# Reordering the front of an attention–MLP kernel around one table load, and finishing the first tiles of each pass in token halves

## The chip, the cores and the metric

The kernel runs on one core of one Trainium2 chip. The metric is the device time of one launch in microseconds (us). Before the change it is 222.36 us, the median of three runs (221.37 to 223.29). The profiled execution of the same kernel spans 220.5 us from its first to its last instruction. All moments below, such as "at 21.91", are us from the start of that span.

A core has five engines that run side by side, each through its own list of instructions in order: TensorE (PE in the profile, and PEld for its weight loads), VectorE (DVE), ScalarE (ACT), GpSimd (POOL) and SyncE (SP, which only issues transfers here). They wait for one another through semaphores.

## What is computed

Two layers follow one another: a chunked attention over four batches of eight heads, and an MLP with a "snake" activation.

```python
# attention: S = 768 tokens in 24 chunks of 32; each chunk sees 16 tokens to its left,
# 8 to its right, and 8 memory rows
scores = (q_c @ k_full.T) / sqrt(64)
out_c  = softmax(scores) @ v_full                 # q, k, v: (4, 8, 768, 64)
x      = out.transpose(0, 2, 1, 3).reshape(3072, 512)

# MLP: d_model 512, d_ff 2048
h = x @ w_in                                      # (3072, 2048)
s = sin(alpha * h)
g = h + s * s / (alpha + 1e-9)
y = g @ w_out                                     # (3072, 512)
```

One batch of 768 tokens is one *pass* of the MLP's first layer, so there are four passes. The 2048 columns of h are cut into 16 *tiles* of 128 (numbered 0 to 15, `ft` in the code). A tile of a pass is 128 partitions by 768 tokens, held as two halves of 384 tokens, each half in a PSUM bank of its own.

## The kernel before

First the work on one tile: eight matmuls into PSUM (four for each token half), the sine on ScalarE, the square on the engine that a letter of a string names (V for VectorE, P for GpSimd, A for ScalarE), and a last step on VectorE that makes g. This last step is called the *snake step* below. It reads the PSUM tile for the last time, so it is also what makes the two banks free for a later tile.

```python
def half_first(hT, ft, hf, xT):                 # 4 matmuls: one token half of one tile
    for kt in range(KT):                        # KT = 4
        nc.tensor.matmul(hT[:, hf, 0:HALF], w_in_sb[:, kt, P * ft:P * ft + P],
                         xT[:, kt, HALF * hf:HALF * hf + HALF], ...)

def ahead(ft, hf, xT):                          # first half of tiles 0 to 2, before the pass
    if ft < 3:
        begun[ft] = two("big")
        half_first(begun[ft], ft, hf, xT)

def first(ft, xT, gT, square, hT=None):
    if hT is None:
        hT = two("h")
        half_first(hT, ft, 0, xT)
    half_first(hT, ft, 1, xT)
    u = mlp.tile([P, 2, HALF], F32, name="u", bufs=4)
    nc.scalar.activation(u[:], hT[:, :, 0:HALF], ACTF.Sin, scale=alpha_sb[:, ft:ft + 1])
    def squared():
        if square == "A":
            nc.scalar.activation(u[:], u[:], ACTF.Square)
        else: ...                               # u * u on VectorE (V) or GpSimd (P)
    def finish():                               # the snake step
        nc.vector.scalar_tensor_tensor(out=gT[:, ft, :]..., in0=u[:],
            scalar=inv_alpha[:, ft:ft + 1], in1=hT[:, :, 0:HALF], op0=ALU.mult, op1=ALU.add)
    return squared, finish
```

The loop of a pass. A snake step is put one tile later in VectorE's list than its tile (two later if GpSimd squares):

```python
for ft in range(FT):
    begin(ft)
    square = squares[ft % len(squares)]
    squared, fin = first(ft, xT, gT, square, begun.pop(ft, None))
    feed.take(...)                              # matmuls of an earlier pass's second layer
    for due, f in [p for p in pend if p[0] <= ft]: f()
    pend = [p for p in pend if p[0] > ft]
    squared()
    pend.append((ft + (2 if square == "P" else 1), fin))
...
layer(0, xT, "VPPAPAVPAVPPAAAA", begin_0, 0)    # pass 0; no second-layer work beside it
layer(i, xT, "VAVAVAVAAVAAVAVA", begin, 0)      # pass 1; none beside it either
layer(i, xT, "AAAV", begin, feed.left() - ...)  # passes 2 and 3, with second-layer matmuls
```

A pass has four pairs of PSUM banks in turn, so tile 4 takes the pair of tile 0, tile 5 that of tile 1, and so on.

The front is the attention of batch 0, worked by pairs of heads and halves of tokens. `sc_half` makes scores and the exponential, `pv` multiplies by v and normalises on VectorE, `x` transposes the result on TensorE and copies it from PSUM to `xT` on ScalarE. `warm(n)` puts n matmuls on zeros into TensorE's list[...]; they write the bank that the next `x` will use. The sine's table has to be loaded on ScalarE between the last exponential and the first sine. The end of the front:

```python
pv(1, 0); sc_half(3, 0); pv(1, 1); sc_half(3, 1)
units = [(hp, half) for hp in range(1, HP - 1) for half in range(2)]
x(1, 0)
nc.scalar.preload_act_table(ACTF.Sin)           # ahead of five more copies on ScalarE
for n in range(2, len(units)):
    pv(*units[n])
    if n == 2:
        warm(2)
    x(*units[n - 1])
warm(1)
pv(3, 0)
x(2, 1)
pv(3, 1)
x(3, 0)
ahead(0, 0, xT)
ahead(1, 0, xT)
x(3, 1)
ahead(2, 0, xT)
```

In the later attentions the table load stands after the last exponential, and `ahead` for tiles 0, 1 and 2 stands among the last transposes.

Of the kernel before, what the change touches and what calls it, by code (L numbers as in the profile page):

```python
# [9 lines left out]
P = 128  # L10
# [4 lines left out]
F32 = mybir.dt.float32  # L15
ACTF = mybir.ActivationFunctionType
ALU = mybir.AluOpType
# [25 lines left out]
def kernel(  # L43
# [12 lines left out]
    nc = tc.nc  # L56
# [5 lines left out]
    HP = H // 2  # L62
# [3 lines left out]
    HALF = S // 2  # L66
# [6 lines left out]
    mlp = ctx.enter_context(tc.tile_pool(name="mlp", bufs=3))  # L73
# [13 lines left out]
    def take_bank(kind):  # L87
        ring = rings[kind]
        bank = next(n for n in ring if n not in kept)
        ring.remove(bank)  # L90
        ring.append(bank)
        return bank

    def two(kind="big"):
        bank = take_bank(kind)
        return ps[:, bank:bank + 2, :]

    def single(kind="one"):
# [27 lines left out]
    alpha_sb = consts.tile([P, FT], F32, name="alpha_sb")  # L126
    inv_alpha = consts.tile([P, FT], F32, name="inv_alpha")
# [132 lines left out]
    def put_k(b, hp, t):  # L260
        kT = kTs[b % 2]
        nc.scalar.copy(  # L262
            kT[:, hp, 72:72 + 7 * 104].rearrange("p (s c) -> p s c", c=104)[:, :, 0:96]
            .rearrange("p s (a r) -> p s a r", r=6),
            t[:, :, 8:120].rearrange("p r (s a) -> p s a r", a=16),
        )
# [66 lines left out]
    def warm(n):  # L333
        z = ps[:, rings["one"][0], :]
        for _ in range(n):
            nc.tensor.matmul(z, idle[:, 0:P], idle[:])  # L336
# [42 lines left out]
        )  # L379
        return x_blk  # L380

    def unit_turn(xT, hp, half, x_blk):
        xtp = packed(single(), 4, QW)
        for jj in range(4):
            nc.tensor.transpose(
                xtp[:, jj, :], x_blk[:, jj].rearrange("p e d -> p (e d)"), ident[0:QW, 0:QW]
            )
        nc.scalar.copy(
            xT[:, hp, HALF * half:HALF * half + HALF].rearrange("p (j c) -> p j c", j=4), xtp
        )  # L390

    def attention_first(kq, alphas, ahead):
        xT = xp.tile([P, KT, S], BF, name="xT")
        pt, xb = {}, {}

        def turn_k(hp):
            t = turn(kq[0], hp, None)
            put_k(0, hp, t)
            put_k_edges(0, hp, t)

        def turn_q(hp):
            put_q(0, hp, turn(kq[1], hp, None))

        def sc_half(hp, half):
            pt[hp, half] = unit_scores(hp, half)

        def sc(hp):
            for half in range(2):
                sc_half(hp, half)

        def pv(*u):
            xb[u] = unit_values(*u, pt[u])

        def x(*u):
            unit_turn(xT, *u, xb.pop(u))

        turn_k(0)
        warm(2)
        turn_q(0)
        mt = packed(single(), HP, 32)  # L420
        for g in range(HP):
            nc.tensor.transpose(mt[:, g, :], memk_bf[0:32, 2 * g:2 * g + 2, :].rearrange("p e d -> p (e d)"), ident[0:32, 0:32])
        nc.vector.tensor_copy(memkT[:], mt)
        put_memk(0)
        warm(3)
        turn_k(1)
        put_memv(0, nc.vector, 0, H)
# [12 lines left out]
        pv(0, 1)  # L440
        t3 = turn(kq[0], 3, None)
        put_k(0, 3, t3)
        warm(1)
        x(0, 0)
        sc_half(2, 0)
        put_k_edges(0, 3, t3)
        turn_q(3)
        sc_half(2, 1)
        x(0, 1)
        warm(1)  # L450
        plan(big=(4, 0, 2))
        pv(1, 0)
        sc_half(3, 0)
        pv(1, 1)
        sc_half(3, 1)
        units = [(hp, half) for hp in range(1, HP - 1) for half in range(2)]
        x(1, 0)
        nc.scalar.preload_act_table(ACTF.Sin)
        for n in range(2, len(units)):
            pv(*units[n])  # L460
            if n == 2:
                warm(2)
            x(*units[n - 1])
        warm(1)
        pv(3, 0)
        x(2, 1)
        pv(3, 1)
        x(3, 0)
        ahead(0, 0, xT)
        ahead(1, 0, xT)  # L470
        x(3, 1)
        ahead(2, 0, xT)
        return xT

    def attention(b, stream, shares, lag, crossed, beside=iter(()), beside_from=0):
# [32 lines left out]
    def half_first(hT, ft, hf, xT):  # L508
        for kt in range(KT):
            nc.tensor.matmul(  # L510
                hT[:, hf, 0:HALF],
                w_in_sb[:, kt, P * ft:P * ft + P],
                xT[:, kt, HALF * hf:HALF * hf + HALF],
                start=(kt == 0), stop=(kt == KT - 1),
            )

    begun = {}

    def ahead(ft, hf, xT):
        if ft < 3:  # L520
            begun[ft] = two("big")
            half_first(begun[ft], ft, hf, xT)

    def first(ft, xT, gT, square, hT=None):
        if hT is None:
            hT = two("h")
            half_first(hT, ft, 0, xT)
        half_first(hT, ft, 1, xT)
        u = mlp.tile([P, 2, HALF], F32, name="u", bufs=4)
        nc.scalar.activation(u[:], hT[:, :, 0:HALF], ACTF.Sin, scale=alpha_sb[:, ft:ft + 1])  # L530

        def squared():
            if square == "A":
                nc.scalar.activation(u[:], u[:], ACTF.Square)  # L534
            else:
                eng = nc.vector if square == "V" else nc.gpsimd
                eng.tensor_tensor(out=u[:], in0=u[:], in1=u[:], op=ALU.mult)  # L537

        def finish():
            nc.vector.scalar_tensor_tensor(  # L540
                out=gT[:, ft, :].rearrange("p (e c) -> p e c", e=2),
                in0=u[:], scalar=inv_alpha[:, ft:ft + 1], in1=hT[:, :, 0:HALF],
                op0=ALU.mult, op1=ALU.add,
            )
        return squared, finish

    def second(i, gT, cut=0):

# [118 lines left out]
    xT = attention_first(kq, alphas, ahead)  # L667
# [14 lines left out]
    def layer(i, xT, squares, begin, to_feed):  # L682
        gT = gTs[i % 2]
        pend = []
        fed = 0
        for ft in range(FT):
            begin(ft)
            square = squares[ft % len(squares)]
            squared, fin = first(ft, xT, gT, square, begun.pop(ft, None))
            want = to_feed * (ft + 1) // FT  # L690
            feed.take(want - fed)
            fed = want
            for due, f in [p for p in pend if p[0] <= ft]:
                f()
            pend = [p for p in pend if p[0] > ft]
            squared()
            pend.append((ft + (2 if square == "P" else 1), fin))
        for due, f in pend:
            f()
        feed.add(second(i, gT, 0 if i else 13), NSUB * FT)  # L700

    prs = []

    def begin_0(ft):
        if ft == 3:
            plan(h=[6] + rings["big"])
        if ft == 12:
            load_v(1)
            send_memv(1)
            send_memv(2)  # L710
        if ft == 15:
            prs.extend(pair_up(kq1[n // HP], n % HP) for n in range(4))
# [6 lines left out]
    for pc in range(2 * HP):  # L719
        hp = pc % HP  # L720
# [12 lines left out]
    xT = attention(1, feed, (6, 8, 4, 4, 4, 3, 3, 3, 3, 1, 1), 2, 5)  # L733

    for i in range(1, B):
# [26 lines left out]
        if not last:  # L762
# [3 lines left out]
            xT = attention(i + 1, feed, (4, 8, 4, 4, 3, 3, 3, 3, 4, 4, 4), 2, 5)  # L766
# [33 lines left out]
```

## Time and profile before

| row of the page or of a view | what it tells |
|---|---|
| PE 209.9 us busy (95%), ACT 147.8 (67%), DVE 136.4 (62%), POOL 83.0 (38%) | TensorE has hardly any idle time over the whole span |
| 80 to 90: PE 9.05, DVE 9.58, ACT 9.49 of 10 us | in pass 1 VectorE and ScalarE are as full as TensorE |
| 120 to 200: PE 20.00 of 20 us in each of the four stretches | from pass 2 on TensorE never stops |
| granted clock of TensorE 0.997 | the clock plays no part |

A row of the timeline gives the start, the time that it lasted, the engine, the line of the kernel, the operation, what it writes and reads, how many instructions were merged into the row, and in brackets how long the engine had stood idle just before and what ended that. A row of the groups gives the busy total and the mean of one instruction in ns. The busy share of an engine is an average over stages with different limits, so the stages have to be read one by one.

### The profile page before, as it was taken

The numbers are of one execution on the slowest core, as the hardware profiler recorded it, in microseconds if no ns is written. First come the engines' busy times: TensorE is split into PE (matmuls) and PEld (weight loads), VectorE is DVE, ScalarE is ACT, GpSimd is POOL, SyncE is SP. The second block draws the span as 40 slices with busy tenths as digits, with TensorE's granted clock in tenths as the row PEclk, the third lists the DMA queues.
The fourth block names the chain that finished last, engine by engine and source line by source line (L and its number), as shares of the span: only waits on it lengthen the run. The fifth ranks groups of instructions, "written<-read, shape, count | busy, mean of one in ns | idle before, by whom it ended". The sixth has DMA issues, their size and how long they took to land.

```text
span 220.5 us, 4412 instructions
## 1 busy us (share of the span) xinstructions
PE 209.9 (95%) x1684; PEld 113.8 (52%) x1684; DVE 136.4 (62%) x234; ACT 147.8 (67%) x217; POOL 83.0 (38%) x102
## 2 busy tenths in 40 slices
PE   7999699999999889999999999999999999999994
PEld 3456455555545555554555555544555555544453
DVE  5867458874527769995872865765854863861110
ACT  2458588895778389999846879797919678660010
POOL 7998653598800599400049179300000000000000
PEclk9999999999999999999999999999999999999998
DMA  5999999999999699996339999996530110101212
GB/s 82 163 165 172 207 207 208 200 174 122 92 198 164 80 159 146 152 175 95 75 86 154 122 110 138 180 218 110 137 116 0 48 52 0 48 37 61 95 48 97
DMA packets 98877, 26.96 MB, mean 122 GB/s; under 512 B 86808, under 2 KB 95912, under 8 KB 98856
## 3 DMA queue, kind: packets, MB, share of 16 engines
q0 software_dynamic: 71520, 14.82, 87.8%
q1 hardware_dynamic: 27336, 11.86, 25.6%
q8 instruction: 13, 0.21, 0.4%
q14 instruction: 8, 0.07, 0.1%
HBM read 29.69 MB, written 6.29 MB: 163 GB/s over the span
## 4 chain that ended last, share of the span: by engine, by line
PE 74%; DVE 10%; DMA 5%; ACT 5%; issue 3%; POOL 1%; DVEq 0%; POOLq 0%
PE ps L556 33%; PE ps L510 27%; DVE gT L540 5%; DMA xT<-x_blk 3%; DVE u L537 3%; PE ps L283 3%; DMA q_bf<-in_q_dram 2%; ACT u L530 2%; PE ps L309 2%; PE ps L579 2%; PE ps L336 1%; PE ps L247 1%; PE ps L341 1%; DVE x_blk L375 1%; PE ps L349 1%
## 5 line engine op out<-in xcount | busy, mean ns | idle before, releaser
L556 PE MATMUL ps<-w_out_sb,gT 128*128 128x512 bf16 x368 | 95.5, 380 | 0.2
L510 PE MATMUL ps<-xT,w_in_sb 128*128 128x384 bf16 x512 | 91.5, 326 | 2.7 <-DVE gT L540 1.3
L540 DVE SCALAR_TENSOR_TENSOR gT<-u,inv_alpha,ps 128x768 bf16<-128x768 f32 x64 | 63.4, 1012 | 24.4 <-ACT u L534 20.8
L530 ACT ACTIVATE u<-ps,alpha_sb 128x768 f32<-128x768 f32 x64 | 56.7, 896 | 27.8 <-PE ps L510 27.1
L510 PEld LDWEIGHTS <-w_in_sb 128*128 128x128 bf16 x512 | 49.4, 98 | 40.9 <-issue 5.8
L556 PEld LDWEIGHTS <-gT 128*128 128x128 bf16 x368 | 32.8, 98 | 29.1 <-issue 0.5
L534 ACT ACTIVATE u<-u 128x768 f32<-128x768 f32 x40 | 33.7, 843 | 1.2
L296 ACT ACTIVATE pt<-ps,biasm 128x256 bf16<-128x256 f32 x72 | 28.7, 473 | 4.6 <-PE ps L283 1.8
L569 DVE COPY o_sb<-ps 128x512 f32<-128x512 f32 x17 | 11.7, 689 | 25.3 <-PE ps L556 25.2
L537 DVE TENSOR_TENSOR u<-u 128x768 f32<-128x768 f32 x18 | 17.1, 952 | 6.0 <-ACT u L530 5.9
L183 POOL DMA_DIRECT2D vw<-in_v_dram x15 | 18.1, 1214 | 0.3 <-issue 0.3
L316 DVE TENSOR_TENSOR x_blk<-ps,rinv 96x512 bf16<-96x512 f32 x24 | 16.5, 687 | 0.8
L143 POOL DMA_DIRECT2D kst<-in_k_dram x16 | 11.1, 691 | 5.2 <-DMA vw<-in_v_dram 5.2
L262 ACT COPY kT<-ps 128x672 bf16<-128x672 bf16 x8 | 5.7, 718 | 9.7 <-PE ps L247 7.2
L571 ACT COPY o_sb<-ps 128x512 f32<-128x512 f32 x6 | 3.5, 584 | 12.7 <-PE ps L556 12.7
L537 POOL TENSOR_TENSOR u<-u 128x768 f32<-128x768 f32 x6 | 9.2, 1546 | 6.5 <-ACT u L530 6.5
L148 POOL DMA_DIRECT2D kst<-in_k_dram x16 | 11.6, 726 | 0.1
L336 PE MATMUL ps<-idle 128*128 128x512 bf16 x27 | 9.0, 448 | 2.3 <-DVE vw L618 1.2
L309 PEld LDWEIGHTS <-pt 128*128 128x128 bf16 x192 | 9.0, 98 | 4.2
L153 POOL DMA_DIRECT2D qst<-in_q_dram x12 | 10.7, 896 | 0.7 <-DMA vw<-memv_st 0.7
L283 PEld LDWEIGHTS <-kT 64*128 64x128 bf16 x192 | 4.9, 94 | 10.4 <-issue 9.9
L315 DVE RECIPROCAL rinv<-ps 96x8 f32<-96x8 f32 x24 | 4.8, 202 | 8.2 <-ACT pt L296 5.2
(81 smaller groups left out, 140.0 us busy)
## 6 DMA issues: line engine op xcount, KB each, us to landing
out_dram<-o_sb SPq DMA_DIRECT2D x23, 256.0 KB
w_out_sb<-in_moe_w_out_dram POOLq DMA_DIRECT2D x2, 1024.0 KB, 18.3
w_in_sb<-in_moe_w_in_dram POOLq DMA_DIRECT2D x3, 512.0 KB, 10.7
vw<-in_v_dram POOLq DMA_DIRECT2D x3, 512.0 KB, 9.2
qst<-in_q_dram POOLq DMA_DIRECT2D x12, 128.0 KB, 6.0
vw<-in_v_dram POOLq DMA_DIRECT2D x2, 448.0 KB, 12.3
kst<-in_k_dram POOLq DMA_DIRECT2D x14, 64.0 KB, 5.3
kst<-in_k_dram POOLq DMA_DIRECT2D x14, 56.0 KB, 5.4
```

The source lines that it names most:

```text
L148: nc.gpsimd.dma_start(kst[72:72 + n, j, :].rearrange("p (h d) -> p h d", d=D), k[b, :, QW * j + 48:QW * j + 48 + n, :].rearrange("h p d -> ...
L183: nc.gpsimd.dma_start(vw[p0:p1, c0:c1, 0:D], flat[r0:r0 + QW * (c1 - c0)].rearrange("(n t) d -> t n d", t=QW)[0:p1 - p0],)
L296: nc.scalar.activation(pt[:, 0:H * QW].rearrange("p (g e c) -> p g e c", g=2, e=4)[:, :, :, 32 * m:32 * m + 32], sc[:, :, 0:4 * QW].rearra ...
L309: nc.tensor.matmul(otv[:, e, hp, :], pt[:, QW * i:QW * i + P], vws[b % 2][:, 2 * hp + e, j, 0:D + 1],)
L316: nc.vector.tensor_tensor(out=x_blk[:].rearrange("p g e d -> p e g d"), in0=otv[0:QW, :, :, 0:D], in1=rinv[:].unsqueeze(3).to_broadcast([Q ...
L510: nc.tensor.matmul(hT[:, hf, 0:HALF], w_in_sb[:, kt, P * ft:P * ft + P], xT[:, kt, HALF * hf:HALF * hf + HALF], start=(kt == 0), stop=(kt ...
L530: nc.scalar.activation(u[:], hT[:, :, 0:HALF], ACTF.Sin, scale=alpha_sb[:, ft:ft + 1])
L534: nc.scalar.activation(u[:], u[:], ACTF.Square)
L537: eng.tensor_tensor(out=u[:], in0=u[:], in1=u[:], op=ALU.mult)
L540: nc.vector.scalar_tensor_tensor(out=gT[:, ft, :].rearrange("p (e c) -> p e c", e=2), in0=u[:], scalar=inv_alpha[:, ft:ft + 1], in1=hT[:, ...
L556: nc.tensor.matmul(ps[:, bank, :], gT[:, ft, P * s:P * s + P], w_out_sb[:, ft, :], start=(ft == 0), stop=(ft == FT - 1),)
L569: nc.vector.tensor_copy(o_sb[:], ps[:, bank, :])
```

## The change

It has two parts. The first moves the load of the sine's table behind the copy of `x(3, 0)`, so that the copies of the front no longer stand behind it in ScalarE's list; the transposes, the value products and the zero matmuls are put in another order (six zero matmuls in this stretch in place of three), `x(3, 1)` is copied by VectorE, and only tiles 0 and 1 are begun ahead of pass 0. The second part lets every tile that is begun ahead of a pass go through sine and square for its first token half at once, both on ScalarE, and through the snake step for that half at the start of the pass; the pass then does only the second half of these tiles. It is meant to bring work forward into time when ScalarE and VectorE are idle, and to shorten what lies between the first matmul of a pass and the first bank that comes free.

```diff
 sc_half(3, 1)
-units = [(hp, half) for hp in range(1, HP - 1) for half in range(2)]
 x(1, 0)
-nc.scalar.preload_act_table(ACTF.Sin)
-for n in range(2, len(units)):
-    pv(*units[n])
-    if n == 2:
-        warm(2)
-    x(*units[n - 1])
+pv(2, 0)
 warm(1)
+x(1, 1)
+pv(2, 1)
+warm(2)
+x(2, 0)
 pv(3, 0)
+warm(2)
 x(2, 1)
 pv(3, 1)
+warm(1)
 x(3, 0)
+nc.scalar.preload_act_table(ACTF.Sin)
 ahead(0, 0, xT)
+x(3, 1, nc.vector.tensor_copy)
 ahead(1, 0, xT)
-x(3, 1)
-ahead(2, 0, xT)
...
 def ahead(ft, hf, xT):
     if ft < 3:
-        begun[ft] = two("big")
-        half_first(begun[ft], ft, hf, xT)
+        hT = two("big")
+        half_first(hT, ft, hf, xT)
+        u = mlp.tile([P, 2, HALF], F32, name="u", bufs=4)
+        e = slice(hf, hf + 1)
+        sine(u, hT, ft, e)
+        nc.scalar.activation(u[:, e], u[:, e], ACTF.Square)
+        begun[ft] = (hT, u)
...
 # first(), squared() and the snake step now work on u[:, e] and hT[:, e]:
 # e is the second half alone for a tile that was begun ahead, else both halves
...
 def layer(i, xT, squares, begin, to_feed):
     ...
+    for ft in sorted(begun):
+        snake(gT, ft, *begun[ft], slice(0, 1))
     for ft in range(FT):
...
 def begin_0(ft):
-    if ft == 3:
-        plan(h=[6] + rings["big"])
+    if ft == 2:
+        plan(h=[rings["big"][0], 6] + rings["big"][1:])
```

The later passes keep their three tiles begun ahead, each with its first half finished early.

More of the change, by code (lines that the diff above doesn't have):

```diff
@@ L380, in unit_values, with unit_turn @@
         return x_blk
-    def unit_turn(xT, hp, half, x_blk):
+    def unit_turn(xT, hp, half, x_blk, copy):
         xtp = packed(single(), 4, QW)
@@ L387, in unit_turn @@
             )
-        nc.scalar.copy(
-            xT[:, hp, HALF * half:HALF * half + HALF].rearrange("p (j c) -> p j c", j=4), xtp
-        )
+        copy(xT[:, hp, HALF * half:HALF * half + HALF].rearrange("p (j c) -> p j c", j=4), xtp)
     def attention_first(kq, alphas, ahead):
@@ L412, in pv, with x @@
             xb[u] = unit_values(*u, pt[u])
-        def x(*u):
-            unit_turn(xT, *u, xb.pop(u))
+        def x(hp, half, copy=nc.scalar.copy):
+            unit_turn(xT, hp, half, xb.pop((hp, half)), copy)
         turn_k(0)
@@ L517, with sine, first, snake @@
     begun = {}
+    def sine(u, hT, ft, e):
+        nc.scalar.activation(u[:, e], hT[:, e, 0:HALF], ACTF.Sin, scale=alpha_sb[:, ft:ft + 1])
     def ahead(ft, hf, xT):
         if ft < 3:
-            begun[ft] = two("big")
-            half_first(begun[ft], ft, hf, xT)
-    def first(ft, xT, gT, square, hT=None):
-        if hT is None:
+            hT = two("big")
[5 more added lines that the diff above has]
+            begun[ft] = (hT, u)
+    def first(ft, xT, square, started=None):
+        e = slice(0, 2)
+        if started is not None:
+            hT, u = started
+            e = slice(1, 2)
+        else:
             hT = two("h")
             half_first(hT, ft, 0, xT)
+            u = mlp.tile([P, 2, HALF], F32, name="u", bufs=4)
         half_first(hT, ft, 1, xT)
-        u = mlp.tile([P, 2, HALF], F32, name="u", bufs=4)
-        nc.scalar.activation(u[:], hT[:, :, 0:HALF], ACTF.Sin, scale=alpha_sb[:, ft:ft + 1])
+        sine(u, hT, ft, e)
         def squared():
             if square == "A":
-                nc.scalar.activation(u[:], u[:], ACTF.Square)
+                nc.scalar.activation(u[:, e], u[:, e], ACTF.Square)
             else:
                 eng = nc.vector if square == "V" else nc.gpsimd
[L537 to L545, printed above, removed]
+                eng.tensor_tensor(out=u[:, e], in0=u[:, e], in1=u[:, e], op=ALU.mult)
+        return hT, u, e, squared
+    def snake(gT, ft, hT, u, e):
+        nc.vector.scalar_tensor_tensor(
+            out=gT[:, ft, :].rearrange("p (e c) -> p e c", e=2)[:, e],
+            in0=u[:, e], scalar=inv_alpha[:, ft:ft + 1], in1=hT[:, e, 0:HALF],
+            op0=ALU.mult, op1=ALU.add,
+        )
     def second(i, gT, cut=0):
@@ L688, in layer @@
             square = squares[ft % len(squares)]
-            squared, fin = first(ft, xT, gT, square, begun.pop(ft, None))
+            hT, u, e, squared = first(ft, xT, square, begun.pop(ft, None))
             want = to_feed * (ft + 1) // FT
@@ L693, in layer @@
             for due, f in [p for p in pend if p[0] <= ft]:
-                f()
+                snake(gT, *f)
             pend = [p for p in pend if p[0] > ft]
             squared()
-            pend.append((ft + (2 if square == "P" else 1), fin))
+            pend.append((ft + (2 if square == "P" else 1), (ft, hT, u, e)))
         for due, f in pend:
-            f()
+            snake(gT, *f)
         feed.add(second(i, gT, 0 if i else 13), NSUB * FT)
```

## The prediction, made before the changed kernel was run

> **What bounds the kernel now.** I read the busy shares of the stretches first, to see which engine limits which stage; then the chain of work that ended last, through the front and the first pass; then TensorE's timeline in pass 1; and last the groups, for the price of one instruction of each kind.
>
> ```profile
> 80.00:90.00 10.00, 9.05 (x54) 5.02 (x53) 9.58 (x12) 9.49 (x12) 10.00 (x15) 1.00 2.10 143
> 90.00:100.00 10.00, 9.94 (x64) 5.56 (x64) 9.42 (x11) 9.56 (x13) 0.63 (x2) 1.00 1.53 161
> 120.00:140.00 20.00, 20.00 (x114) 11.01 (x113) 14.18 (x16) 16.64 (x21) 14.05 (x19) 1.00 2.37 129
> ```
>
> The columns are the busy us of PE, PEld, DVE, ACT and POOL. In pass 1 (75 to 101) VectorE and ScalarE are full. From 120 to 200 TensorE alone is full, in each stretch of 20 us, so there time can go only with TensorE's work, and the change takes none away from passes 2 and 3. What it can win lies before 101.
>
> ```profile
> 21.91 1.28 ACT L458
> 23.20 0.49 ACT xT L388
> 23.73 0.38 PE ps L336
> 24.71 0.70 DVE x_blk L375
> 25.46 0.36 PE ps L385 x4
> 25.84 0.49 ACT xT L388
> 26.37 0.97 PE ps L510 x5
> 27.51 1.32 PE ps L510 x8
> 28.85 0.91 ACT u L530
> 29.79 0.97 DVE u L537
> 30.86 1.02 DVE gT L540
> 31.93 5.47 PE ps L510 x32
> ```
>
> This is the chain at the front's end. The load of the sine's table is on it: the copies of x stand behind it, a zero matmul waits 1.11 us for their bank, then value product, normalising and the last copies follow. At 28.85 the first sine starts; sine, square and snake step of tile 0, each on 768 columns, take until 31.87, and tile 4, which needs tile 0's banks, starts at 31.93. TensorE had stood 0.51 us.
>
> ```profile
> 77.34 3.41 PE L510 MATMUL ps<-xT,w_in_sb 128*128 128x384 bf16 x20 [0.22 <-DVE xT L329]
> 81.25 5.67 PE L510 MATMUL ps<-xT,w_in_sb 128*128 128x384 bf16 x32 [0.50 <-DVE gT L540]
> 89.98 7.96 PE L510 MATMUL ps<-xT,w_in_sb 128*128 128x384 bf16 x48 [0.15 <-DVE gT L540]
> ```
>
> In pass 1 TensorE runs from 77.34 to 97.94, 20.60 us for the 116 matmuls left after the three halves ahead. One takes 0.163 us in a stream (24 in 4.07 us at 27.35, of which about 0.33 is the last one's whole length), so 18.9 us of work and 1.7 of waiting for VectorE's snake steps.
>
> ```profile
> L540 DVE SCALAR_TENSOR_TENSOR gT<-u,inv_alpha,ps 128x768 bf16<-128x768 f32 x64 | 63.4, 1012 | 24.4 <-ACT u L534 20.8
> L530 ACT ACTIVATE u<-ps,alpha_sb 128x768 f32<-128x768 f32 x64 | 56.7, 896 | 27.8 <-PE ps L510 27.1
> L534 ACT ACTIVATE u<-u 128x768 f32<-128x768 f32 x40 | 33.7, 843 | 1.2
> L537 DVE TENSOR_TENSOR u<-u 128x768 f32<-128x768 f32 x18 | 17.1, 952 | 6.0 <-ACT u L530 5.9
> ```
>
> These are the prices of a whole tile: snake step 1012 ns, sine 896, square 843 on ScalarE and 952 on VectorE (GpSimd 1546).
>
> [...] The trace has the 1283 (the row at 21.91) [...]: the next copy starts at 23.20, 0.01 us after the load's end. So I count 1.28 us and no more. [...] the trace has 896 and 843. So half a tile costs more than half: [...] 320 ns less, which is 576 ns for a sine and 523 for a square (estimates from 896 and 843). [...] the trace has 952. For 384 I take 400 ns off: 552 for a square, and 612 for a snake step (from 1012). [...] The two halves of a tile lie in two banks, so TensorE may fill one while ScalarE reads the other. No run yet shows this overlap inside one tile.
>
> **The front, step by step.** I lay the new order on the durations above. Up to 21.2 nothing changes. Then, with no table load in the way: copy (1,1) on ScalarE ends at 22.35, where the old trace has 23.7; pv(2,1) and two zero matmuls end at 22.4, as copy (1,0) freed their bank at 21.90; x(2,0) at 22.4, its block being ready at 22.23; pv(3,0) at 22.56; two zero matmuls, then x(2,1) at 23.2; pv(3,1) at 23.4; x(3,0) at 24.05, when its block is normalised. VectorE's normalisations, 0.93 us a pair of instructions, are now the steps that the rest waits for. Copy (3,0) ends at 24.95 instead of 26.32: 1.37 us earlier, the 1.28 of the load and a little. The three extra zero matmuls (0.21 us each) lie in gaps.
>
> Then the load, 24.95 to 26.23, stands before the first sine. Meanwhile TensorE does tile 0's first half (its last matmul waits for copy (3,0), as before), x(3,1), tile 1's first half (to 26.0), the second halves of tiles 0 and 1 (x(3,1) copied by VectorE at 25.86), and tiles 2 and 3 whole, done at 29.9 instead of 31.42.
>
> ScalarE after the load, at about 0.53 us for each half operation in a row: sine and square of tile 0's half, the same for tile 1, then the second-half sines: tile 0's ends near 28.95, tile 1's near 29.5, whole sine 2 at 30.4, sine 3 at 31.3. Square of half 0 on VectorE 0.55, snake half 0.61: banks of tile 0 free at 30.2. Tile 4 starts at about 30.25, where TensorE was ready at 29.9. Against 31.93 that is **1.7 us earlier**. ScalarE itself is only 1.0 us earlier (sine 3 ends 31.3 against 32.35), since it has two squares more (1.05 us) and two sines in halves (2 x 576 - 896 = 256 ns each), but it has 1.8 us of waits for TensorE between 33 and 44 to make that up.
>
> Through the rest of pass 0 the waits stay about the same: in the old trace 96 matmuls took 16.27 us where a stream needs 95 x 0.163 + 0.33 = 15.8. In the new order the bank of tile 2 (whole square on GpSimd, 1.55 us, done near 32.05) costs 0.3 us at tile 6. I put the end of pass 0 **1.5 us earlier**, at 46.6.
>
> **Between the passes.** The attention of batch 1 begins with turned k and q. The transfer of q was issued at 24.63 and took 26.2 us to land, so it lands at 50.8 whatever the engines do; GpSimd first reads it at 52.97. A gain of up to 2.1 us passes; 1.5 does. The load of v lands at about 59.4, and its last part is first read at 64.65. The sum stays 1.5 us.
>
> **Pass 1.** Shown on the old clock. The table is loaded by 73.89 and ScalarE idles until 78.18, so three half sines and squares fit in: tile 0's half is in PSUM at 75.26, tile 2's at 77.11; the six operations end near 78.6. VectorE does the three half snake steps between 77.3 and 79.2, where it had almost nothing. In the pass proper VectorE then has, instead of 16 snake steps and 7 squares (16 x 0.95 + 7 x 0.88 = 21.4 us in its stream), 13 whole and 3 half steps, 5 whole and 2 half squares: 12.4 + 1.7 + 4.4 + 1.0 = 19.5. That is 1.9 less. ScalarE has 13 whole and 3 half sines, 8 whole and 1 half squares from 78.6: about 13 x 0.85 + 3 x 0.53 + 8 x 0.83 + 0.5 = 19.8, ending at 98.4; in the old trace it ends at 99.83. So VectorE stops being the limit, ScalarE becomes it, and TensorE's waits (1.7 us) nearly vanish. The next attention's first exponentials come **1.4 us earlier**, as do the matmuls.
>
> **Passes 2 and 3.** TensorE-bound: nothing won. ScalarE's extra work, three squares and three split sines in each, about 2 us, falls after the exponentials, where it waits 5.0 us for TensorE (117.77 is its first sine). **0 us.**
>
> Sum: 1.5 + 1.4 + 0 = 2.9 us of 222.36, which is **219.4 us**.
>
> **The rivals.** First, ScalarE takes the place of VectorE and of the load: the moved load now stands straight before the first sine, and ScalarE gets about 1.5 us more work in pass 0. For it speaks that ScalarE is busy 20 of 22 us there. Against it speaks the 1.8 us of slack. If it ruled, pass 0 would win 0.7 us and pass 1 perhaps 0.8: 220.9. Second, the time won in pass 0 is given back at a transfer: q of batch 1, or the crossings of k and q for batch 2, which SyncE issues one after another until 102.03. For it speaks that neither moves with ScalarE. Against it, q has 2.1 us to spare, and the crossings are released by x of the pass before, so they shift with it, and the last is used after 109. It would leave about 1.4 of the sum: 221.0. Third, it goes better: the shorter first path takes out all of the 0.45 us of waits in pass 0 and all of 1.7 in pass 1, with the front's whole 1.7: 1.7 + 0.4 + 1.7 = 3.8, 218.6. Beyond 2% (217.9) I'd need a gain after 101, where TensorE is full.
>
> **Range and chances.** The three rivals span 218.6 to 221.0; the three runs of before differ by 1.9 us, so I widen by about 0.6 below and 0.3 above: 218.0 to 221.3. Faster by over 2% needs all that the third rival gives and 0.7 us more: 0.12. Slower by over 2% needs a new wait of 7 us, for which I see no source: 0.03. Within 2%: 0.85.
>
> **What would show it.** Right: the table load near 24.9 with no zero matmul waiting for a copy; tile 4 at 30.0 to 30.5; second-layer matmuls of pass 0 from about 46.5; in pass 1 no wait of TensorE above 0.2 us at tile 4, and VectorE's share of those 20 us below ScalarE's; from 120 on the same rows, shifted. Wrong: sines queueing behind one another with TensorE waiting for VectorE early in pass 0 (first rival); GpSimd's copies of q, or scores, waiting for a transfer (second rival); TensorE with gaps in passes 2 and 3, where I expect no change.

## The result and the profile after

| | before | after |
|---|---|---|
| median time, us (6 executions each) | 222.41 | 219.62 |
| range, us | 221.37 to 223.45 | 218.23 to 220.68 |
| ratio, 95% interval | | 0.987 (0.982 to 0.992) |
| span of the profiled execution, us | 220.5 | 218.1 |
| busy us: TensorE, VectorE, ScalarE, GpSimd | 209.9, 136.4, 147.8, 83.0 | 210.9, 137.7, 153.0, 82.4 |

The change takes 1.3% off; 219.4 was predicted. To see where, I cut the span of TensorE's timeline at its own milestones. "Front and pass 0" runs from the transposes of x(1,0) to the first second-layer matmul. "Pass 1" and "pass 2" run from a pass's first matmul to the first scores of the next attention. The "turns" into passes 1, 2 and 3 run from the first scores of an attention to the first matmul of that pass. "Rest" is from the first matmul of pass 3 to the last matmul's end. The 12.12 us from the first second-layer matmul to the first scores of batch 1 are the same in both traces and are left out. All in us:

| kernel | x(1,0) at | front and pass 0 | turn to 1 | pass 1 | turn to 2 | pass 2 | turn to 3 | rest |
|---|---|---|---|---|---|---|---|---|
| before | 20.61 | 27.42 | 14.30 | 24.95 | 14.37 | 33.37 | 13.73 | 56.39 |
| after | 21.39 | 25.70 | 13.50 | 23.58 | 14.01 | 33.33 | 14.80 | 56.32 |
| gain | -0.78 | 1.72 | 0.80 | 1.37 | 0.36 | 0.04 | -1.07 | 0.07 |

The first column isn't the change's doing: another execution of the kernel before reached x(1,0) at 21.37, and a kernel with the new front reached it at 20.69. Two stages give 3.1 us together, two turns 1.16, and the third turn takes 1.07 back.

The busy times by stretch of the changed kernel (columns: PE, PEld, DVE, ACT, POOL, granted clock, DMA share, GB/s):

```profile
80.00:90.00 10.00, 9.99 (x62) 5.94 (x61) 9.08 (x11) 9.80 (x12) 9.63 (x14) 1.00 2.13 144
90.00:100.00 10.00, 9.73 (x68) 4.80 (x68) 8.69 (x10) 9.88 (x16) 0.07 (x1) 1.00 1.69 149
120.00:140.00 20.00, 20.00 (x115) 11.05 (x113) 13.30 (x15) 16.13 (x20) 12.35 (x17) 1.00 2.49 140
```

VectorE has fallen from 9.58 and 9.42 of 10 to 9.08 and 8.69. ScalarE is now the fuller of the two (9.80 and 9.88), and TensorE is busy 9.99 of the first 10 instead of 9.05. From 120 on TensorE is as full as it was.

The chain of work that ended last, at the end of the front (pieces under 0.36 us left out):

```profile
21.49 0.81 ACT pt_first L356
22.30 0.38 ACT xT L388
22.73 0.59 PE ps L336 x2
23.73 0.43 PE ps L336 x2
24.83 0.36 PE ps L385 x4
25.24 0.47 issue
25.71 1.28 ACT L467
27.00 0.59 ACT u L518
27.64 0.41 issue
28.05 0.57 ACT u L518
28.67 0.40 issue
29.07 1.04 ACT u L518 x2
30.19 2.26 POOL u L547 x2
32.47 1.02 DVE gT L551
33.54 2.77 PE ps L508 x16
```

The load (L467, 25.71) stands alone now: the copies are ahead of it, and no zero matmul waits 1.11 us for a bank. The first sine starts at 27.00, 0.01 us after the load's end. The trace has four loads of the sine's table, 1283 ns each, one between the last exponential and the first sine of each pass (L467 once, L482 three times); no run leaves one out.

TensorE's timeline; the number in brackets is the idle time before the row:

```profile
25.01 1.05 PE L508 MATMUL ps<-xT,w_in_sb 128*128 128x384 bf16 x4
26.07 21.18 PE L508 MATMUL ps<-xT,w_in_sb 128*128 128x384 bf16 x124
...
75.61 19.24 PE L508 MATMUL ps<-xT,w_in_sb 128*128 128x384 bf16 x116 [0.22 <-DVE xT L329]
...
158.43 0.81 PE L508 MATMUL ps<-xT,w_in_sb 128*128 128x384 bf16 x4 [0.92 <-DMA xT<-x_blk]
```

A row runs on over idle times under 0.15 us. The 124 matmuls of pass 0 form one row, where the old trace had a stop of 0.51 us. Pass 1's 116 take 19.24 us in one row instead of 20.60 in four. The last row is the turn to pass 3: a wait of 0.92 us for a transfer that transposes x. The old trace has none there:

```profile
160.86 0.81 PE L510 MATMUL ps<-xT,w_in_sb 128*128 128x384 bf16 x4
```

The groups by shape, for the half operations (count, then busy total and mean in ns):

```profile
L551 DVE SCALAR_TENSOR_TENSOR gT<-u,inv_alpha,ps 128x384 bf16<-128x384 f32 x22 | 13.1, 611 | 5.3 <-ACT u L527 2.9 <-ACT u L544 2.0
L518 ACT ACTIVATE u<-ps,alpha_sb 128x384 f32<-128x384 f32 x22 | 12.4, 571 | 5.4 <-PE ps L508 4.9
L527 ACT ACTIVATE u<-u 128x384 f32<-128x384 f32 x11 | 5.8, 523 | 0.3
```

The estimates for these were 612, 576 and 523 ns.

### The profile page after: what moved, and what is told of

The parts are those of the page before. It is cut to its first block, busy times and chain, and to the rows that moved or that the text cites. A ratio compares the mean times of both kernels' runs of the same rounds, so it can differ in the third digit from the quotient of the medians.

```text
span 218.1 us, 4457 instructions
## 1 busy us (share of the span) xinstructions
PE 210.9 (97%) x1687; PEld 114.6 (53%) x1687; DVE 137.7 (63%) x246; ACT 153.0 (70%) x238; POOL 82.4 (38%) x102
## 4 chain that ended last, share of the span: by engine, by line
PE 80%; DVE 6%; ACT 6%; issue 3%; POOL 2%; DMA 2%; DVEq 0%; ACTq 0%
PE ps L566 35%; PE ps L508 27%; PE ps L336 4%; ACT u L518 3%; PE ps L283 3%; DVE gT L551 3%; PE ps L309 2%; POOL u L547 2%; DMA xT<-x_blk 2%; PE ps L247 2%; PE ps L589 2%; PE ps L341 1%; DVE u L547 1%; PE ps L349 1%; PE ps L244 1%
## 5 line engine op out<-in xcount | busy, mean ns | idle before, releaser
L551 DVE SCALAR_TENSOR_TENSOR gT<-u,inv_alpha,ps 128x768 bf16<-128x768 f32 (+1 forms) x75 | 65.8, 895 | 22.9 <-ACT u L544 16.1
L518 ACT ACTIVATE u<-ps,alpha_sb 128x768 f32<-128x768 f32 (+1 forms) x75 | 59.4, 800 | 20.3 <-PE ps L508 19.7
L544 ACT ACTIVATE u<-u 128x768 f32<-128x768 f32 (+1 forms) x40 | 31.5, 787 | 1.2
L547 DVE TENSOR_TENSOR u<-u 128x768 f32<-128x768 f32 (+1 forms) x18 | 15.9, 886 | 1.7 <-ACT u L518 1.6
L336 PE MATMUL ps<-idle 128*128 128x512 bf16 x30 | 10.9, 477 | 1.3 <-DVE vw L628 1.2
L547 POOL TENSOR_TENSOR u<-u 128x768 f32<-128x768 f32 (+1 forms) x6 | 8.7, 1463 | 6.4 <-ACT u L518 6.4
```

The lines of the kernel that those rows point to most:

```text
L518: nc.scalar.activation(u[:, e], hT[:, e, 0:HALF], ACTF.Sin, scale=alpha_sb[:, ft:ft + 1])
L544: nc.scalar.activation(u[:, e], u[:, e], ACTF.Square)
L547: eng.tensor_tensor(out=u[:, e], in0=u[:, e], in1=u[:, e], op=ALU.mult)
L551: nc.vector.scalar_tensor_tensor(out=gT[:, ft, :].rearrange("p (e c) -> p e c", e=2)[:, e], in0=u[:, e], scalar=inv_alpha[:, ft:ft + 1], i ...
```

## The experiments

Theory: pass 0 gains through the new front alone; pass 1 gains because VectorE has less to do inside the pass; the 1.07 us lost at pass 3 come from something that the change brings in. Rivals: that the halves win in pass 0 too; that in pass 1 only the first bank's release counts; that the loss is chance. All medians below stand beside the kernel before in the same batch of runs (222.6 to 222.9).

**Each part alone.** The first kernel keeps the new front and finishes no tile early.

```diff
-def ahead(ft, hf, xT):
+def ahead(ft, hf, xT, early=True):
...
+    u = None
+    if early:
         u = mlp.tile(...); sine(u, hT, ft, e); ...Square
...
-ahead(0, 0, xT)
+ahead(0, 0, xT, False)      # and so at all five calls
```

> Only the front is reordered (table load behind the copy of x(3,0), x(3,1) copied by VectorE); no tile is finished early in any pass. Theory (the load on the path cost 1.28 us, and TensorE is ready for tile 4 about 1.5 us earlier without it): from the transposes of x(1,0) to the first second-layer matmul 25.5 to 25.9 us, as in the changed kernel (25.70; before 27.42), and pass 1 from its first matmul to the next scores 24.9 as before (24.95). Time 220.4 to 221.0. Rival (the halves are what shortens pass 0, since they shorten sine, square and snake step of tile 0): this stretch 26.8 to 27.4, time 221.8 or more.

Measured: 221.41 us, ratio 0.994 (0.992 to 0.996). The time lies above the 220.4 to 221.0 expected, which left out the wait at pass 3 (1.10 us here). Front and pass 0 take 25.72, pass 1 takes 24.95 as in the kernel before. Its TensorE timeline in pass 1 still has the stop for the first bank:

```profile
76.15 3.41 PE L508 MATMUL ps<-xT,w_in_sb 128*128 128x384 bf16 x20 [0.22 <-DVE xT L329]
80.06 2.76 PE L508 MATMUL ps<-xT,w_in_sb 128*128 128x384 bf16 x16 [0.50 <-DVE gT L556]
```

The second kernel finishes the first halves early and has the front of before, except that VectorE copies x(3,1).

```diff
 x(1, 0)
+preload_act_table(Sin)             # the order of before:
+... pv(n), warm(2), x(n - 1) ... warm(1), pv(3, 0), x(2, 1), pv(3, 1), x(3, 0)
 ahead(0, 0, xT)
-x(3, 1, nc.vector.tensor_copy)
 ahead(1, 0, xT)
+x(3, 1, nc.vector.tensor_copy)
+ahead(2, 0, xT)
```

> The front of before with the table load where it was; the tiles begun ahead are finished by halves in every pass (x(3,1) is copied by VectorE so that it does not stand behind the early sines). Theory: the first stretch gains at most the 0.5 us wait at tile 4, 26.9 to 27.4 us; pass 1 takes 23.4 to 23.8 us instead of 24.95, as in the changed kernel (23.58). Time 220.6 to 221.2. Rival (halves shorten pass 0): first stretch 26.0 or less, time under 220.

Measured: 220.45 us, ratio 0.990 (0.986 to 0.993). Front and pass 0 take 27.11, only 0.31 less than before; pass 1 takes 23.59, the whole of its gain. So the new front makes pass 0's gain and the halves make pass 1's. This kernel has no wait at pass 3 (turn to 3: 13.73); the first has one of 1.10 us. The gains of the two medians, 1.49 and 2.45 us, add to more than the change gives, because the kernel before had a lower mean clock in 17 of its 27 executions here (see the last experiment), which enters both. Against the other ten, with a median of 222.19, they are 0.78 and 1.74.

**The halves of pass 0 in the new front.** `ahead(0, 0, xT, False)` and `ahead(1, 0, xT, False)` in the front only; the later passes as in the change.

> The changed kernel without early halves in pass 0 only. Theory: the halves do nothing in pass 0, because ScalarE starts late there and pays two extra squares and two split sines: first stretch 25.5 to 25.9 us, pass 1 23.4 to 23.8, time within 0.5 us of the changed kernel (219.6). Rival (halves are needed in pass 0): first stretch above 26.3, time 220.4 or more.

Measured: 220.24 us, ratio 0.988 (0.985 to 0.992); front and pass 0 take 25.70, exactly the change's. Busy times by stretch, first of this kernel, then of the changed one:

```profile
24.00:30.00 6.00, 5.89 (x51) 3.60 (x50) 3.27 (x7) 4.43 (x6) 2.77 (x5) 1.00 1.24 206
30.00:36.00 6.00, 5.68 (x35) 3.22 (x34) 4.58 (x6) 5.00 (x7) 4.20 (x3) 1.00 1.24 207
36.00:42.00 6.00, 6.00 (x39) 3.61 (x38) 5.58 (x6) 4.98 (x7) 1.90 (x2) 1.00 1.30 202
42.00:48.00 6.00, 6.00 (x36) 3.33 (x35) 4.94 (x5) 5.51 (x7) 6.00 (x5) 1.00 1.37 202
```

```profile
24.00:30.00 6.00, 5.89 (x51) 3.59 (x50) 3.32 (x8) 5.18 (x11) 2.39 (x4) 1.00 1.25 207
30.00:36.00 6.00, 5.85 (x37) 3.42 (x36) 4.48 (x7) 5.89 (x8) 3.72 (x3) 1.00 1.24 207
36.00:42.00 6.00, 5.95 (x37) 3.49 (x36) 5.60 (x6) 4.59 (x6) 2.30 (x2) 1.00 1.30 202
42.00:48.00 6.00, 5.89 (x36) 3.26 (x34) 4.89 (x5) 5.50 (x7) 6.00 (x5) 1.00 1.37 202
```

Without the halves TensorE stops 0.32 us at tile 5 (5.68 of 6 in the second stretch). With them it stops less in that stretch (5.85, at tile 6), and in small pieces later (5.95 and 5.89 instead of 6.00 twice). The sums are 23.57 and 23.58: the halves move a short stop and win nothing. With the load out of the way TensorE has only about 0.4 us of 24 left to lose.

**The halves of passes 2 and 3.** Early halves only in passes 0 and 1 (`ahead(ft, 0, xT, b == 1)` in the attentions).

> The changed kernel with early halves in passes 0 and 1 only, none in passes 2 and 3. Theory: passes 2 and 3 are full of matmuls, the halves win nothing there: within 0.4 us of the changed kernel (219.6). Rival: early halves also help there, or their work on ScalarE and VectorE disturbs the last transposes and costs the 0.9 us wait for x seen at the start of pass 3: then 0.5 to 1 us slower or faster than 219.6.

Measured: 219.77 us, ratio 0.987 (0.983 to 0.990), with a pass 2 of 33.37 and a rest of 56.31. The halves of the last two passes are worth nothing, as predicted.

**How many halves pass 1 needs.** In the attentions only tile 0 is finished early; tiles 1 and 2 are begun as in the kernel before. If all that counts is the first bank's release, tile 0 is enough. If it is VectorE's work inside the pass, a third of the halves gives about a third of the gain.

> The changed kernel with only tile 0 finished early in passes 1 to 3 (tiles 1 and 2 are begun ahead, as before, but do sine, square and snake step whole inside the pass). Theory (pass 1 is limited by the sum of VectorE's work, and the gain is the work taken out of it): tile 0 carries about half of the 1.9 us, so pass 1 takes 24.2 to 24.6 us, between 24.95 without halves and 23.58 with three tiles. Rival (the gain is the first bank coming free sooner, which tile 0 alone decides): pass 1 23.5 to 23.8 us, as with three tiles.

Measured: 220.74 us, ratio 0.992 (0.989 to 0.995); pass 1 takes 24.48, a gain of 0.47 out of 1.37.

```profile
75.86 6.01 PE L508 MATMUL ps<-xT,w_in_sb 128*128 128x384 bf16 x36 [0.22 <-DVE xT L329]
82.22 13.78 PE L508 MATMUL ps<-xT,w_in_sb 128*128 128x384 bf16 x80 [0.35 <-DVE gT L556]
```

The stop after 20 matmuls (0.50 us in the kernel before) is gone, since tile 0's banks come free in time; the next, after 36, is 0.35 us. A third of the halves gives 0.34 of the gain (0.47/1.37), so the rival falls. A finer rival is that each half frees the banks of its own tile sooner. But in the kernel before TensorE also stops at tiles 8 and 10 (0.31 us each, from start to start), whose banks are freed by tiles 4 and 6. In the changed kernel those two are done whole, and yet the first stop is gone and of the second 0.17 us is left. What fits both is the work taken out of VectorE's list ahead of them.

**The wait at pass 3.** First I ran both kernels again for a second trace of each.

> The changed kernel once more, for a second trace. Theory: the stretch from x(1,0) to the second layer 25.7 us and pass 1 23.6 us again; the 0.9 us wait for the transposed x at the start of pass 3 returns, because every kernel with the new front had it (0.76 to 1.10 us in four traces) and the two with the old front had none. Rival (chance of the transfers): the wait is absent this time.

> The kernel before once more, for a second trace of it. Theory: 27.4 us from x(1,0) to the second layer, 24.95 in pass 1, and no wait for the transposed x at the start of pass 3. Rival (chance): a wait of about 1 us there now and then, as in the changed kernel.

Measured: the changed kernel 219.99 us, ratio 0.988 (0.984 to 0.992), with waits of 0.40 us at pass 2 and 0.47 at pass 3; the kernel before, 222.61 in one execution, with 0.36 at pass 1 and none at pass 3. So the wait at pass 3 came back, with another size. What the wait is for can be read in SyncE's timeline of the changed kernel, in which it issues the transfers:

```profile
150.70 5.10 SPq L492 DMA_TRANSPOSE xT<-x_blk  x4
155.90 1.40 SPq L582 DMA_DIRECT2D out_dram<-o_sb  x1
157.39 1.21 SPq L492 DMA_TRANSPOSE xT<-x_blk  x1
```

The first half of x needs the four transposes issued until 155.80, and an output's transfer lies before the fifth. I took that output for the cause and moved the outputs of attentions to GpSimd's list.

```diff
-nc.sync.dma_start(out[...], o_sb[:])
+eng = nc.gpsimd if state["attending"] else nc.sync
+eng.dma_start(out[...], o_sb[:])
```

> The changed kernel with the output tiles that fall inside an attention sent by GpSimd instead of SyncE, so that SyncE's list between the transposes of x holds nothing else. Theory: the last transposes of x are issued 0.5 to 1.5 us sooner, the wait of 0.9 us at the start of pass 3 goes, and the time falls by 0.5 to 1.2 us against the changed kernel, to 218.5 to 219.2. Rival (the transposes themselves are slow then, whoever is in front of them): the wait stays and the time is the same within 0.4 us.

Measured: 221.84 us, ratio 0.997 (0.994 to 0.999); the wait grew to 1.80 us at pass 3 and a new one of 0.85 came at pass 2. SyncE's five transposes in a row, in this kernel:

```profile
152.09 7.15 SPq L492 DMA_TRANSPOSE xT<-x_blk  x5
```

The first four end 5.14 us after their start, at 157.23, as long as in the changed kernel (5.10); the fifth takes 1.92. With no output in between the wait is still there, so the theory of the output fell.

Next I looked at what the DMA engines move when the fourth transpose lands. The queues of the changed kernel from 155.5 to 156, as packets, MB, and share of the engines:

```profile
q1 hardware_dynamic: 98, 0.03, 26.0%
q8 instruction: 1, 0.02, 13.6%
```

A single packet of 16 KB, of the queue of instructions, falls on the last of the four transposes. Every trace has 13 such packets (0.21 MB) over its span. This one in each kernel's trace, to half a us, beside the end of the fourth transpose's issue:

| kernel | six TensorE instructions more? | fourth transpose issued until | the packet, in | wait at pass 3 |
|---|---|---|---|---|
| before | no | 159.14 | 161.0 to 161.5 | none |
| halves alone | no | 156.30 | 158.5 to 159.0 | none |
| after | yes | 155.80 | 155.5 to 156.0 | 0.92 |
| after, again | yes | 155.95 | 156.0 to 156.5 | 0.47 |
| new front alone | yes | 157.76 | 157.5 to 158.0 | 1.10 |
| tile 0 alone | yes | 157.22 | 157.0 to 157.5 | 1.37 |
| halves of passes 0 and 1 | yes | 156.81 | 157.0 to 157.5 | 0.96 |
| no halves in pass 0 | yes | 156.45 | 156.0 to 156.5 | 0.76 |
| before, again | no | 159.21 | 160.5 to 161.0 | none |
| outputs by GpSimd | yes | 157.23 | 157.5 to 158.0 | 1.80 |

Where the packet comes within 0.8 us of the fourth transpose there is a wait, and where it comes 1.3 us later or more there is none. The kernels with the wait have three zero matmuls more, each a weight load and a matmul: six more instructions in TensorE's list. The page of the changed kernel has two queues of instructions:

```profile
q8 instruction: 13, 0.21, 0.4%
q14 instruction: 8, 0.07, 0.1%
```

Their bytes stand about as 3 to 1, as do TensorE's instructions (3374 of 4457 on the page) to those of the other engines, so q8 may well carry TensorE's list. Then six instructions more could bring a packet forward. That can be tested both ways: three zero matmuls fewer in the changed kernel, three more in the kernel before.

```diff
 pv(2, 1)
-warm(2)
+warm(1)
 x(2, 0)
 pv(3, 0)
-warm(2)
+warm(1)
 x(2, 1)
 pv(3, 1)
-warm(1)
 x(3, 0)
```

> The changed kernel with three zero matmuls fewer at the end of the front, so with as many TensorE instructions in all as the kernel before. Theory (the wait for x at the start of pass 3 comes from a fetch of TensorE's instructions, 16 KB at a time, that falls onto the last transposes of x; the six instructions more of the new front moved it there): the stretch from x(1,0) to the second layer stays 25.7 us, since the zero matmuls lay in gaps; the fetch falls later, the stretch from the scores to pass 3 goes from 14.4 to 14.8 back to about 13.8 us, time 0.5 to 1 us under the changed kernel (219.6 to 220.0). Rival (the wait depends on when the stretch begins, not on the count): it stays at 14.4 or more and the time is the same.

Measured: 219.19 us, ratio 0.983 (0.980 to 0.987). Front and pass 0 take 25.69 as in the change, so those zero matmuls did lie in gaps there; and no turn shows a wait for a transposed x. TensorE at the turn to pass 3, SyncE before it, and the DMA queues from 157 to 157.5, in this kernel:

```profile
156.85 0.81 PE L507 MATMUL ps<-xT,w_in_sb 128*128 128x384 bf16 x4
```

```profile
149.75 5.09 SPq L491 DMA_TRANSPOSE xT<-x_blk  x4
154.94 0.53 SPq L581 DMA_DIRECT2D out_dram<-o_sb  x1
155.56 1.20 SPq L491 DMA_TRANSPOSE xT<-x_blk  x1
```

```profile
q8 instruction: 1, 0.02, 13.7%
```

The packet comes 2.2 us or more after the fourth transpose's issue (154.84), and the output's issue takes 0.53 us instead of 1.40. The other way round, in the kernel before:

```diff
 if n == 2:
-    warm(2)
+    warm(5)
```

> The kernel before with three zero matmuls more in its front, where TensorE waits for the table load anyway: six TensorE instructions more, as in the changed kernel, and nothing else. Theory (fetch of instructions): the stretch from x(1,0) to the second layer stays 27.4 us, but the stretch from the scores to pass 3 goes from 13.7 to 14.4 or more; time 0.5 to 1 us above the kernel before. Rival: 13.7 us as before and the same time within 0.3 us.

Measured: 223.12 us, ratio 1.001 (0.999 to 1.004). The medians of all executions don't resolve it. Among those at full clock it is 0.65 us more (223.12 of 13 against 222.47 of 11), as the theory had it. And the trace has what was to appear, the first matmul of pass 3 with a wait; below it is the same matmul in the second trace of the kernel before:

```profile
162.23 0.81 PE L510 MATMUL ps<-xT,w_in_sb 128*128 128x384 bf16 x4 [1.08 <-DMA xT<-x_blk]
...
161.18 0.81 PE L510 MATMUL ps<-xT,w_in_sb 128*128 128x384 bf16 x4
```

The packet lies between 159.5 and 160 here, the fourth transpose's issue ends at 159.26. The kernel before, once more, reached x(1,0) at 21.37, as this one does (21.36), has the same front and pass 0, and has no wait. So the later start alone isn't the cause. But this rests on that one trace, for all eight traces with the wait reach x(1,0) at 21.36 to 21.51, and the other five without it, that with three fewer among them, at 20.53 to 20.69.

Shown: with the six instructions the wait is there in all eight traces, without them in none of six (two of the six come with the next experiment). The transposes land late and aren't only issued late: from the end of the fourth one's issue to pass 3's first matmul it is 2.48 to 3.20 us in the eight, and at most 2.39 in the six. Inferred: that the packet is TensorE's own program and that it holds up the last transpose. No run moved the packet without changing TensorE's list. How six instructions move it so far is open, too: it comes after TensorE's weight load 1374 in the kernel before and after 1357 in the changed one, 17 earlier, where three were added.

**The zero matmuls of the old front, and the clock.** The record of all executions shows a granted clock of 0.989 to 0.992 in 40 of 79 of the kernel before, with a median of 223.3 us, against 222.1 for the other 39. Of the varied kernels one execution had it. I suspected TensorE's gaps in the old front (the trace of before has a clock of 1.00 there, from 20 to 25), took its three zero matmuls away, and ran the kernel before once more for its trace.

```diff
-            if n == 2:
-                warm(2)
             x(*units[n - 1])
-        warm(1)
         pv(3, 0)
```

> The kernel before without the three zero matmuls among the last copies of the front; nothing else is changed. In the runs so far the kernel before has in about half of its executions (40 of 79) a mean granted TensorE clock of 0.989 to 0.992, and those take 223.3 us in the median against 222.1 for the others; of 93 timed executions of the varied kernels one has it. Theory: TensorE's gaps in the front (3.43 us busy of the 5 between 20 and 25, where the changed kernel has 4.78) let the clock fall there for some us, and the zero matmuls are only just enough to keep it up. Then nearly all executions here have the low mean clock, the median is 0.4 to 0.9 us above the kernel before's, and the trace has a granted clock well below 1.00 in a stretch between 22 and 35. Rival: the low clock has nothing to do with this place (the end of the kernel, or the chip at that moment). Then about half of the executions have it, as before, and the time is within 0.3 us of before's. With six TensorE instructions fewer than before I expect no wait for the transposed x at pass 3, as in the kernel before, though the packet of instructions should come later still, so this is open.

> The kernel before once more, for its trace. In about one of two such executions the mean granted clock should be near 0.991. If it is, the theory says that the clock is below 1.00 between 22 and 35 and full elsewhere, and that the time from x(1,0) to the first second-layer matmul is about 28.6 us instead of 27.42; the rival says that the low clock lies elsewhere. If the mean is near 1.00 this execution tells nothing of the place.

Measured: the kernel without them takes 221.15 us, ratio 0.993 (0.990 to 0.995), and 3 of 18 executions had the low clock, against 7 of 21 of the kernel before in that batch. The theory fell: it said nearly all. The other trace (221.76 us) had a mean of 0.998 and tells nothing of the place. Neither trace has a wait at pass 3, as expected. But the time fell where I expected it to rise. TensorE's timeline of the kernel without the zero matmuls:

```profile
22.21 0.34 PE L385 MATMUL ps<-ident,x_blk 96*128 96x96 bf16 x4 [0.54 <-DVE x_blk L375]
22.39 0.41 PE L368 MATMUL ps<-vw,pt_first 128*128 128x65 bf16 x8
23.66 0.33 PE L385 MATMUL ps<-ident,x_blk 96*128 96x96 bf16 x4 [0.87 <-ACT xT L388]
23.83 0.41 PE L368 MATMUL ps<-vw,pt_first 128*128 128x65 bf16 x8
```

Front and pass 0 take 26.45 us, 0.97 less than before, with the load where it was. The value product pv(3,0) now starts at 22.39 instead of about 23.95. A zero matmul writes the bank of the next x, so it had to wait for the copy behind the load, and pv(3,0), which needs no copy, stood behind it in TensorE's list. So more than half of what the new front wins in the first stretch (0.97 of 1.72) comes with the load where it was, by taking out three zero matmuls. They went together; it is the timeline that points to the last.

## Why the prediction was right, and where it wasn't

- **Pass 0, 1.5 us: right, measured 1.72.** The load was to come at 24.95 and came at 25.71, which is 24.93 once the 0.78 us of the later start is taken off. The second layer was to start at 46.5; it starts at 47.09, or 46.31. The 0.3 given back at tile 6 came true: its first matmul starts at 33.54, 0.48 us after the one before it, where a stream has 0.163, because tile 2's snake step ends at 33.49. What I had too dear was tile 4. I let it wait for both banks of tile 0, until 30.25; its first matmuls need only the first half's bank, which the half snake step frees at 28.79, and they start at 30.63 (29.85 without the later start), with no stop. Two things in the working were credited wrongly. I laid out the halves of pass 0 operation by operation as part of the gain; the run without them shows that they earn nothing there. And I booked the gain to the load; the kernel without the old zero matmuls gets 0.97 of it with the load unmoved. No run moved the load alone.
- **1.28 us for the load and no more: right.** It takes 1283 ns in both traces, and here the first sine itself starts 0.01 us after the load's end.
- **Pass 1, 1.4 us: right, measured 1.37,** for the reason given. VectorE's share falls below ScalarE's, and a third of the halves gives a third of the gain. ScalarE becomes the fullest beside TensorE without holding it up (9.80 of 10 us from 80 to 90, where TensorE has 9.99). The 1.7 us of waits were counted a little high: worked out as for pass 0 (115 x 0.163 + 0.33 = 19.1) they are 1.5, of which the change leaves about 0.2.
- **The price of halves: right** within 5 ns for sine, square and snake step, and for the square on VectorE (552 expected, 551 measured). The 320 ns less on ScalarE can be read in the trace of before, though in copies alone: out of PSUM they take 799 ns for 768 columns and 479 for 384. No trace of before shows the 400 ns less on VectorE; in the changed kernel a half takes 401 ns less than a whole in the snake step (611 against 1012) and 402 in the square (551 against 953). No run had yet shown TensorE and ScalarE in the two banks of one tile at once. Here ScalarE reads the first half of tile 0 from 27.00 to 27.58 while TensorE, from 26.73 on, fills the second. Ten matmuls start from 26.07 to 27.58, one in 0.163 us as in a stream, so the trace shows no wait from it.
- **Passes 2 and 3, 0 us: right for the passes** (0.04 and 0.07), **wrong for the turn to pass 3.** "The three extra zero matmuls lie in gaps" holds in the front and not in the program: with six instructions more there is a wait of 0.47 to 1.80 us some 135 us later. The sum came out by luck, because another term was missing too. The turns to passes 1 and 2 were 0.80 and 0.36 us shorter, mostly because waits of 0.63 and 0.21 us for a transposed x were absent in this trace of the changed kernel. Such waits come and go between executions of one kernel (0.36 and 0.40 in the second traces); I didn't settle what brings them. In the second traces of both kernels the three turns give 0.36, -0.38 and -0.64 us, so there the turns take back 0.66 of the 3.1.
- **The rivals.** ScalarE did not take VectorE's place as a limit, and q of batch 1 landed in time: issued at 24.34, it took 26.0 us, to about 50.3, and GpSimd first read it at 52.03. The third rival's reason holds in part: pass 1 has lost its stops, but 1.7 there was too much.
- **Not foreseen:** the kernel before runs at a lower mean clock in half of its executions. Its median is 0.3 us above that of its full-clock ones (222.41 against 222.1), so about that part of the 2.8 us between the medians is this and no step of mine. In the batch that ran the change again it is more: 219.99 stands against 222.73 for all executions of the kernel before and against 221.97 for those at full clock, a gain of 2.0 us. That the measured 2.8 meets the predicted 2.9 so closely is in part luck.

The best version is the change with three zero matmuls fewer: 219.19 us, ratio 0.983 (0.980 to 0.987) to the kernel before. Against the change it was not run in one batch; the intervals of the two ratios overlap.

## What to carry to other kernels

Put a table load (1.28 us here) behind the last copy that other engines wait for, and give filler matmuls a bank that no pending copy still reads: here a zero matmul waited 1.11 us for its bank, and pv(3,0) behind it started at about 23.95, against 22.39 in the kernel without the old front's zero matmuls. Finishing a part of a tile before a stage paid here in the one stage that VectorE limited (1.37 us in pass 1) and not in the three others of the changed kernel; count the operations that it takes out of the limiting engine's list there. When a wait turns up far from an edit, compare the traces' DMA queues at that moment before looking for a dependency.

## What the runs showed of the hardware

- With six instructions more in TensorE's list a 16 KB packet of an instruction queue came within 0.8 us of the last of four DMA transposes instead of 1.3 us or more after it, and the matmul that needs them waited 0.47 to 1.80 us. That the packet causes the wait is inferred.
- A DMA transpose keeps SyncE 1.18 to 2.33 us in the traces of the kernel before and the changed one, with medians by tile of 1.21 to 1.25, and four of x in a row 5.09 to 5.14. The fifth ahead of pass 3 took 1.21 in these two and 1.82 to 2.30 in some others, among them the one with outputs by GpSimd (1.92).
- The time of x(1,0) differs by 0.8 us between executions of one kernel (20.61 and 21.37). The spread is there at TensorE's first 11 zero matmuls (4.03 and 4.88 us): in one trace they start 0.43 us apart until 4.16 and then 0.21 to 0.25, in the other all of them at about 0.43. So a comparison of two traces by absolute times has to take it off.
- A mean granted clock near 0.991 goes with about 1.2 us in the kernel before (medians of 223.3 and 222.1). Of the varied kernels only the two with the old front and no early halves had it (1 of 14 executions with three zero matmuls more, 3 of 18 with three fewer). No trace caught it, so where it lies and why stays open.
